# A fused attention and two-layer MoE kernel on one Trainium2 core: partial token sums kept as one running sum, a second double bank for scores, five buffers for float64 weights

## The chip, the core and the metric

The kernel runs on one core of one Trainium2 chip. TensorE (PE) multiplies, with a weight load (PEld) ahead of each matmul; VectorE (DVE), ScalarE (ACT) and GpSimd (POOL) do the elementwise work; SyncE (SP) issues every DMA of this kernel, one after the other in one queue. SBUF holds 128 partitions. PSUM has eight banks, into which PE writes; here a bank holds 512 float32 numbers in each partition. The metric is the device time of one execution in microseconds (us).

## The reference

Batch 4, 12 heads, 448 tokens, head size 64; the first expert layer is 768 x 2048, the second has 32 slots for 8 experts of 1024. All inputs are float32 but two: `w_in` and `w_out` carry a factor that numpy keeps in float64 and reach the kernel as 64-bit words.

```python
scores = scale * q @ k.T;  causal mask;  attn = softmax(scores);  x = attn @ v     # per head
x = concatenate the heads                                                         # [4*448, 768]
h = x @ w_in;  g = h * clip(h + 3, 0, 6) / 6;  y = g @ w_out                      # 768 -> 2048 -> 768
logits = y @ phi                                                                  # [1792, 32]
d = exp(logits - max over tokens) / (sum over tokens + 1e-9)
slot_input = d.T @ y                                                              # [32, 768]
slot_out[e] = maximum(slot_input[e] @ w1[e], 0) @ w2[e]                           # 8 experts, 4 slots each
c = softmax of logits over slots;  out = c @ slot_out                             # [1792, 768]
```

## The kernel before

**Stages.** Attention runs over 24 pairs of heads (6 for each batch). The first expert layer runs over 64 units, 16 feature tiles of 128 for each of the 4 batches: one unit is 18 matmuls (L734, both operands split into a high and a low part, three products of six row blocks), a ReLU on ACT (L739), a product on DVE (L741) and, for batches 1 to 3, a 32 x 32 block transpose (L745) into `gtok`, which holds a batch's `g`. `y` is never formed: `phi` is multiplied into `w_out` beforehand (`wp`), so four units at a time give logits (L767), and `d.T @ g` (`U`) is multiplied by `w_out` once, at the end.

**Float64 weights.** Each of 32 blocks of `w_out` and `w_in` is loaded as 64-bit words into one of three `raw` buffers, turned into float32 by ACT and three DVE operations (L627 to L639), and stored back to DRAM as float32 (`wo_d`, `wi_d`). Units of batches 1 to 3 load `wi_d`.

**Token sums.** For batch 0 `U` is a plain product (L939). For batches 1 and 2, 56 small matmuls of 512 columns (`ublocks`, L785) leave four partial sums in four PSUM banks, and four DVE operations add them to four partial sums in SBUF (`U4`, 128 x 2048), each scaled by `c1(SAL)`. After the last batch eight such DVE operations (L857) follow, and then, for eight pieces in turn, PE adds up and transposes the parts (L1045, L1049), DVE copies the piece to `wp` (L1054) and PE multiplies it by `w_out` (L1062).

**Second layer.** `w1` and `w2`, 64 loads of 768 KB, pass through buffers named `ring`. These are laid into SBUF as earlier stages leave it: `RINGS` says how many at each of eight points, in the order start, `cv_end` (conversions over), `a_end` (attention over), `b_end` (batch 2 over), `x_end` (last unit's weights read), `h_end` (last unit multiplied), `g_end` (users of the `g` buffers done), `m_end` (users of `gtok` done); five more come at `o_end`, when the product with `w_out` is done. A load that has no buffer holds up the SP queue behind it.

**Order.** The program has no fixed order: every step is put into a `Schedule` with engine, assumed cost, dependencies, buffers and a priority made from the table `TU`, and a list scheduler writes all instructions in the order it finds. It also writes throwaway matmuls (L390, `filler`) where it expects PE to be idle. PSUM: three `h` banks for units and logits, one double bank `ps` for scores (a pair needs it four times), one `o`, two `t` for transposes. Attention of batch 0 uses `t`; later pairs are transposed on DVE and by DMA (`xd`).

## Time and profile before

| | |
|---|---|
| runs | 656.09, 655.76, 654.37 us; median 655.76 |
| profiled execution | 655.37 us, of which the span is 653.5 |
| granted TensorE clock, mean | 0.958 |
| busy: PE, DVE, ACT, POOL | 594.8, 407.5, 250.4, 150.6 us |
| moved by DMA | 144.59 MB, mean 221 GB/s |

Busy times of engines overlap, so they don't add up to the span. Where an engine waits, the trace names the one that released it. PE busy also counts the throwaway matmuls. A granted clock of 1.00 is 2.4 GHz, 0.50 is 1.2 GHz.

### The profile page before, as it was taken

What the parts mean: (1) busy time and instruction counts of PE and PEld (TensorE: products, weight loads), DVE (VectorE), ACT (ScalarE), POOL (GpSimd) and SP (SyncE); (2) the same over time, 40 slices, a digit from 0 to 9 for tenths busy, and PEclk for the clock granted to TensorE, in tenths of its full rate; (3) what the DMA queues carried; (4) which work ended last, traced back from release to release, by engine and by line L of the source; (5) the groups of instructions that cost most, each with busy time, mean ns of one, the idle gap of its engine ahead of it and who ended that gap; (6) DMA issues with size and microseconds to landing.
All of it is one profiled execution on the core that took longest, in us unless ns stands there. A gap on an engine that the chain in (4) does not pass through costs nothing.

```text
span 653.5 us, 14639 instructions
## 1 busy us (share of the span) xinstructions
PE 594.8 (91%) x5816; PEld 446.1 (68%) x5816; DVE 407.5 (62%) x948; ACT 250.4 (38%) x420; POOL 150.6 (23%) x212
## 2 busy tenths in 40 slices
PE   7799899988988889999999999999999999998582
PEld 5688676766877678758878777888788654463021
DVE  6889888679886796787686867555655423010032
ACT  2466556445455554524344541433333201110032
POOL 1234446424462222323234322210000010000000
PEclk8899999899998999999999999999999999879877
DMA  7998878879879789872676543279833449999987
GB/s 205 314 294 254 217 213 207 189 168 241 171 199 252 171 194 249 219 168 76 121 164 125 135 91 79 73 206 402 314 97 97 174 175 416 415 414 414 393 291 252
DMA packets 196244, 144.59 MB, mean 221 GB/s; under 512 B 154704, under 2 KB 174672, under 8 KB 196176
## 3 DMA queue, kind: packets, MB, share of 16 engines
q1 hardware_dynamic: 196176, 143.66, 74.5%
q8 instruction: 46, 0.75, 0.5%
q14 instruction: 22, 0.18, 0.1%
HBM read 121.41 MB, written 22.22 MB: 220 GB/s over the span
## 4 chain that ended last, share of the span: by engine, by line
PE 45%; DMA 12%; DVE 10%; SPq 2%; ACT 2%; issue 2%; DVEq 0%; ACTq 0%
PE ph L734 25%; DMA ring<-in_moe_w_dram 8%; DMA raw<-in_moe_w_in_dram 3%; DVE ps L491 3%; PE ps L526 2%; SPq L406 2%; PE t L1124 2%; PE o L564 2%; PE pl L767 1%; PE t L785 1%; PE ps L1109 1%; PE pl L734 1%; PE ph L1109 1%; PE ps L476 1%; PE o L1062 1%
## 5 line engine op out<-in xcount | busy, mean ns | idle before, releaser
L734 PE MATMUL ph<-xp,wpl 128*128 128x448 f32 x1098 | 238.3, 372 | 2.4 <-DVE wpl L723 2.3
L734 PEld LDWEIGHTS ph<-xp,wpl 128*128 128x128 f32 x1098 | 204.0, 189 | 32.7 <-issue 8.7
L739 ACT ACTIVATE r<-ph,three 128x448 f32<-128x448 f32 x61 | 38.6, 632 | 124.0 <-PE ph L734 119.3
L549 POOL TENSOR_SCALAR_AFFINE_SELECT s<-s 128x256 f32<-128x256 f32 x96 | 49.6, 540 | 145.4 <-ACT s L541 140.1
L741 DVE SCALAR_TENSOR_TENSOR g<-r,ph 128x448 f32<-128x448 f32 x61 | 37.5, 614 | 55.4 <-ACT r L739 52.4
L491 DVE CUSTOM_DVE_ANT_0 ps<-ps,maskw 128x448 f32<-128x448 f32 (+3 forms) x144 | 61.7, 428 | 15.1 <-PE ps L476 10.5
L725 POOL TENSOR_TENSOR wpl<-cx,wpl 128x768 fp32r<-128x768 f32 x26 | 49.8, 1916 | 80.7 <-ACT wpl L720 74.8
L720 ACT ACTIVATE wpl<-cx 128x768 fp32r<-128x768 f32 x64 | 53.6, 838 | 29.6 <-PE ph L734 16.0
L526 PE MATMUL ps<-qp,kp 64*64 64x64 f32 (+3 forms) x576 | 58.2, 309 | 6.7 <-DVE mc L491 2.7
L541 ACT ACTIVATE s<-ps 128x896 f32<-128x896 f32 (+2 forms) x72 | 50.0, 731 | 28.6 <-PE ps L531 25.8
L526 PEld LDWEIGHTS ps<-qp,kp 64*128 64x128 f32 (+1 forms) x576 | 42.4, 177 | 22.5 <-ACT s L541 5.1
L564 PE MATMUL o<-vr,s 128*64 128x65 f32 (+1 forms) x1536 | 53.6, 224 | 0.0
L564 PEld LDWEIGHTS o<-vr,s 128*64 128x64 f32 (+1 forms) x1536 | 48.6, 137 | 5.0 <-issue 2.9
L627 ACT ACTIVATE ca<-raw 128x768 f32<-128x768 f32 x32 | 29.4, 919 | 46.8 <-DMA raw<-in_moe_w_in_dram 26.3
L723 DVE TENSOR_TENSOR wpl<-cx,wpl 128x768 fp32r<-128x768 f32 x38 | 35.8, 943 | 3.9 <-ACT wpl L720 3.6
L476 PE MATMUL ps<-kp,qp 64*128 64x448 f32 (+1 forms) x192 | 27.3, 342 | 11.5 <-DVE mc L495 4.0
L745 DVE STREAM_TRANSPOSE gtok<-g 128x448 f32<-128x448 f32 x48 | 29.7, 632 | 4.0 <-PE ps L785 3.1
L636 DVE SCALAR_TENSOR_TENSOR cw<-ca,cw 128x768 uint32<-128x768 uint32 x32 | 30.7, 958 | 2.2 <-ACT ca L627 0.7
L476 PEld LDWEIGHTS ps<-kp,qp 64*128 64x128 f32 x192 | 14.4, 173 | 23.9 <-issue 10.1
L630 DVE TENSOR_SCALAR cw<-raw 128x768 uint32<-128x768 uint32 x30 | 18.7, 622 | 19.0 <-DMA raw<-in_moe_w_in_dram 11.1
L531 PE MATMUL ps<-dg,oner 64*128 64x448 f32 (+1 forms) x192 | 28.4, 295 | 0.0
L1215 PE MATMUL o<-ring,wos 128*32 128x384 f32 x108 | 21.3, 627 | 5.7 <-DMA ring<-in_moe_w_dram 5.7
(236 smaller groups left out, 802.0 us busy)
## 6 DMA issues: line engine op xcount, KB each, us to landing
ring<-in_moe_w_dram SPq DMA_DIRECT2D x54, 768.0 KB, 14.6
cx<-wi_d SPq DMA_DIRECT2D x48, 384.0 KB, 3.5
...
wos<-in_moe_w_dram SPq DMA_DIRECT2D x10, 768.0 KB, 15.1
...
```

The source lines that it names most:

```text
L476: nc.tensor.matmul(ps.t[:n, h, c:c + w], pl["q"].t[r, 0, q0:q0 + n], pl["k"].t[r, 0, 0:w], start=(t == part[0][0]), stop=adds, skip_group_ ...
L491: nc.vector.tensor_tensor_reduce(out=x, in0=x, in1=maskw[:n, 320 - q0:320 + n] if t else maskw[:n, 320:320 + n], scale=-1.0, scalar=3.0e38 ...
L526: nc.tensor.matmul(ps.t[:kn, h, col:col + n], pl["k"].t[r, x, q0:q0 + kn], pl["q"].t[r, y, q0:S], start=(c == 0 and col == 0), stop=False, ...
L541: nc.scalar.activation(out=o, in_=x, func=ACTF.Exp, scale=SCALE)
L549: nc.gpsimd.affine_select(out=x, in_=x, pattern=[[0, 2], [1, kn]], compare_op=ALU.is_ge, fill=0.0, base=0, channel_multiplier=-1)
L564: nc.tensor.matmul(o.t[64 * h:64 * h + 64, VD * j:VD * j + VD], s.t[:kn, h, c:c + 64], vr.t[:kn, h, t, :], start=(t == 0), stop=(t == ts[- ...
L720: e = sc.add("ACT", 0.84, lambda w=w, cx=cx: nc.scalar.activation(out=w.t[:, 0], in_=cx.t, func=ACTF.Copy), [cr], [cx, w], ps_)
L723: ("DVE", 1.0, lambda w=w, cx=cx: nc.vector.tensor_sub(w.t[:, 1], cx.t, w.t[:, 0].bitcast(F32))),
L725: ("POOL", 2.0, lambda w=w, cx=cx: nc.gpsimd.tensor_sub(w.t[:, 1], cx.t, w.t[:, 0].bitcast(F32))),
L734: nc.tensor.matmul(h.t[:, :S], w.t[:, a, kk, :], x.t[:, c, kk, :], start=(n == 0), stop=(n == len(seq) - 1))
L739: rr = sc.add("ACT", 0.63, lambda h=h, r=r: nc.scalar.activation(out=r.t, in_=h.t[:, :S], func=ACTF.Relu, bias=three), [hh], [h, r], pr - ...
L741: gg = sc.add("DVE", 0.62, lambda h=h, r=r, g=g: nc.vector.scalar_tensor_tensor(out=g.t, in0=r.t, scalar=6.0, in1=h.t[:, :S], op0=ALU.min, ...
```

## The change

Three edits to the computation. (1) For batches 1 to 3 the four partial sums are copied to SBUF by ACT or DVE (into a part of `gtok` whose use is over), added up by four PE matmuls of `sel4`, and one DVE operation scales and adds the result into one running sum `U` (`collect`); `U4` is gone. For the last batch this is done in two halves of 256 columns; each half is then transposed on DVE straight into `wp`, and the product with `w_out` follows. Batch 0's `U` is brought into the same layout by four more PE transposes and three DVE operations. (2) The two `t` banks become one double tile `pt`; once all users of `t` are done it joins the pool `ps` as a second double bank. The logits are transposed to `ltok` by eight DVE transposes for a batch instead of PE transposes, for batches 1 to 3; the ReLU is written into `g`, so the pool `r` is gone. (3) `raw` has five buffers. `g_end` now waits for users of `g`, `zT` and `ls`. The scheduler is told the kind of each PE step (the whole array, `full`, or tiles of it), prefers a step of the kind last run (`KEEP`) and counts a turn between kinds (`TURN`); costs of loads and steps and most of `TU` have other values.

```diff
-TU = {'PO': [-130.96, -7.26, -2.82, -5.86], 'TO': [11.72, -10.42, 32.02, 147.16], 'PB': 0.63, 'AB': -1.38, 'TB': 194.0, 'DUTY': 0.6, 'RINGS': [1, 4, 2, 3, 1, 6, 2, 3], 'LOOK': 0.49, 'FILL': 0.96, 'RAW': 3, 'CA': 1, 'CW': 1, 'S': 2, 'PAIR': 12.99, 'UNIT': 4.99, 'WP0': 35.23, 'WPS': 7.75, 'T0': 216.97, 'L0': -2.47, 'L1': -0.16, 'GP': 201.12, 'TP': 4.91, 'ZP': 38.03, 'UP': 36.81, 'P0': 14.01, 'NQ': 2, 'WAIT': 0.09, 'AHEAD': 2.19, 'LAT': 0.23, 'CX': 2, 'G': 5, 'R': 1, 'VR': 2, 'XT': 2, 'Q': 1, 'AS': 1.42, 'A1': -27.02, 'A2': 6.86, 'A3': 17.6, 'A4': -15.86, 'A5': 3.85, 'A6': 27.35, 'A7': 16.05, 'DG': 2, 'DV': 6, 'TT': 2, 'LO': 1.77, 'DA': 6, 'DX': 6}
+TU = {'KEEP': 2.63, 'PO': [-133.04, -17.63, -10.01, -36.65], 'TO': [8.22, 2.26, 22.67, 165.17], 'PB': 0.68, 'AB': -0.37, 'TB': 219.67, 'DUTY': 0.6, 'RINGS': [0, 6, 2, 4, 1, 5, 2, 3], 'LOOK': 0.65, 'FILL': 0.96, 'RAW': 5, 'CA': 1, 'CW': 1, 'S': 2, 'PAIR': 12.84, 'UNIT': 4.71, 'WP0': 32.06, 'WPS': 6.3, 'T0': 212.76, 'L0': -15.91, 'L1': -14.62, 'GP': 199.53, 'TP': 0.97, 'ZP': 85.68, 'UP': 95.27, 'P0': 15.86, 'NQ': 2, 'WAIT': 0.09, 'AHEAD': 3.2, 'LAT': 0.23, 'CX': 2, 'G': 5, 'R': 1, 'VR': 2, 'XT': 2, 'Q': 1, 'AS': 1.42, 'A1': -10.9, 'A2': 7.25, 'A3': 45.16, 'A4': -24.35, 'A5': -8.06, 'A6': 29.73, 'A7': 16.15, 'DG': 2, 'DV': 6, 'TT': 2, 'LO': -17.05, 'DA': 6, 'DX': 6}
...
-                x = min((x for x in c if x[0] <= t0 + self.WAIT), key=lambda x: (x[1].prio, x[1].n))
+                x = min((x for x in c if x[0] <= t0 + self.WAIT), key=lambda x: (
+                    x[1].prio + (self.KEEP if x[2][1] == "PE" and x[1].full != self.full else 0.0), x[1].n))
...
-                cost = self.array(t, cost, s.weight)
+                cost = self.array(t, cost + (self.TURN if s.full != self.full else 0.0), s.weight)
+                self.full = s.full
...
-        many(mog, TU["R"], "r", [P, S])
...
-        ptt = many(pst, 2, "t", [P, 512])
+        ptt = pst.tile([P, 2, 512], F32, name="pt")
+        sc.pool("t", [ptt[:, 0], ptt[:, 1]])
...
-                h, r, g, x = sc.buf("h"), sc.buf("r"), sc.buf("g"), xb[b]
+                h, g, x = sc.buf("h"), sc.buf("g"), xb[b]
...
+                hh.full = True
+                rr = sc.add("ACT", 0.63, lambda h=h, g=g: nc.scalar.activation(
+                    out=g.t, in_=h.t[:, :S], func=ACTF.Relu, bias=three), [hh], [h, g], pr - TU["GP"])
+                gg = sc.add("DVE", 0.62, lambda h=h, g=g: nc.vector.scalar_tensor_tensor(
+                    out=g.t, in0=g.t, scalar=6.0, in1=h.t[:, :S], op0=ALU.min, op1=ALU.mult), [rr], [h, g], pr - TU["GP"])
...
-            def ublocks(banks, zT):
+            def ublocks(banks, zT, f0=0, nf=KF):
...
-                            banks[i][o:o + 32, :], zT.t[r, 32 * j:32 * j + 32], ug[r, :, 32 * j:32 * j + 32],
+                            banks[i][o:o + 32, :32 * nf], zT.t[r, 32 * j:32 * j + 32],
+                            ug[r, f0:f0 + nf, 32 * j:32 * j + 32],
...
+            def collect(banks, bufs, um, up, c0, n, deps, pr, v0=0):
+                part = gflat[:, c0:c0 + 4 * n].rearrange("p (i x) -> p i x", i=4)
+                ev = []
+                for i in range(4):
+                    ev.append(sc.any([
+                        ("ACT", 0.16 + n * 0.84e-3, lambda i=i: nc.scalar.activation(
+                            out=part[:, i], in_=banks()[i][:, :n], func=ACTF.Copy)),
+                        ("DVE", 0.1 + n * 1.04e-3, lambda i=i: nc.vector.tensor_copy(part[:, i], banks()[i][:, :n])),
+                    ], [um], bufs, pr))
+
+                def total():
+                    for i in range(4):
+                        nc.tensor.matmul(
+                            up()[32 * i:32 * i + 32, :n], sel4[:, 0, :], part[:, i],
+                            start=True, stop=True, tile_position=(0, 32 * i))
+
+                m = sc.add("PE", 0.2 + n * 1.7e-3, total, ev, bufs, pr)
+                return sc.add("DVE", 0.1 + n * 1.04e-3, lambda: nc.vector.scalar_tensor_tensor(
+                    out=U[:, v0:v0 + n], in0=U[:, v0:v0 + n], scalar=c1(SAL), in1=up()[:, :n],
+                    op0=ALU.mult, op1=ALU.add), [m] + deps, bufs, pr), ev
...
-                zT, idS = sc.buf("zT"), sc.buf("g")
...
-                ub, u2 = [sc.buf("t") for _ in range(2)], sc.buf("ps", False)
-                banks = lambda: [ub[0].t, ub[1].t, u2.t[:, 0], u2.t[:, 1]]
-                um = sc.add("PE", 3.7, lambda: ublocks(banks(), zT), [zd] + lasts, [gtb, zT, u2] + ub, T1)
+                ldone = logits_out(lr, [la], T1 + 2)
+                ua, ub = [sc.buf("ps") for _ in range(2)], [sc.buf("h") for _ in range(3)] + [sc.buf("o")]
                 u_part = []
-                for hf in range(2):
-                    cs = slice(8 * hf, 8 * hf + 8)
-
-                    def uadd(cs=cs):
-                        for i in range(4):
-                            nc.vector.scalar_tensor_tensor(
-                                out=U4[:, cs, i], in0=U4[:, cs, i], scalar=c1(SAL), in1=blk(banks()[i])[:, cs],
-                                op0=ALU.mult, op1=ALU.add)
-
-                    u_part.append(sc.add("DVE", 1.4, uadd, [um, sal, s0, prev_u], ub + [u2], T1 + hf))
+                for hf, bufs in enumerate((ua, ub)):
+                    def banks(hf=hf):
+                        return [u.t for u in ub] if hf else [u.t[:, x] for u in ua for x in range(2)]
+
+                    um = sc.add("PE", 2.2, lambda hf=hf, banks=banks: ublocks(banks(), zT, 8 * hf, 8),
+                                [zd] + lasts, [gtb, zT] + bufs, T1 + 3 * hf)
+                    u, ev = collect(banks, [gtb] + bufs, um, lambda banks=banks: banks()[0], hf * DFF * 7 // 4, 256,
+                                    [sal, prev_u], T1 + 3 * hf + 1, 256 * hf)
+                    u_part.append(sc.add("DVE", 0.38, lambda hf=hf: nc.vector.transpose(
+                        wp[:, 8 * hf:8 * hf + 8, :].rearrange("p f s -> p (f s)"), U[:, 256 * hf:256 * hf + 256]),
+                        [u], [], T1 + 3 * hf + 1))
+                    if not hf:
+                        si, si_free = ua[1], ev
...
+                ub = [sc.buf("ps") for _ in range(2)]
+                banks = lambda ub=ub: [u.t[:, x] for u in ub for x in range(2)]
+                bufs = [gtb] + ub
+                a = sc.add("PE", 4.3, lambda banks=banks, zT=zT: ublocks(banks(), zT), [zd] + lasts,
+                           [zT] + bufs, T0 + UNIT * KF - TU["UP"])
+                prev_u, _ = collect(banks, bufs, a, lambda ub=ub: ub[0].t[:, 0], 0, 512, [prev_stat, prev_u], pr)
...
+        def t_end():
+            sc.free["t"].clear()
+            sc.grant("ps", ptt)
+
+        sc.add("SP", 0.0, t_end, sc.users("t"), [], 0)
...
-        ge = sc.add("SP", 0.0, g_end, [he] + sc.users("g", "r", "ls"), [], 0)
+        ge = sc.add("SP", 0.0, g_end, [he] + sc.users("g", "zT", "ls"), [], 0)
...
-        si = sc.buf("o")
         smm = None
-        for hf in range(2):
-            for c in range(4):
-                up = sc.buf("h")
-                j0 = 2 * hf
-
-                def utr(up=up, c=c, j0=j0):
-                    nc.tensor.matmul(
-                        up.t[:, :64], U[:, c * P:(c + 1) * P], idS.t[:, 32 * j0:32 * j0 + 64],
-                        start=True, stop=False, skip_group_check=True)
-                    for j in range(2):
+        for m in range(KF // 2):
+            def simm(m=m):
+                for d in range(2):
+                    for r in range(2):
+                        g = d * 2 + r
                         nc.tensor.matmul(
-                            up.t[:, 32 * j:32 * j + 32], U4[:, 4 * (j0 + j) + c].rearrange("p i x -> p (i x)"),
-                            sel4[:, 0, :], start=False, stop=(j == 1), skip_group_check=True)
-
-                a = sc.add("PE", 0.4, utr, [u_part[hf]], [up, idS], T1 + 4 * hf + c)
-                a = sc.add("DVE", 0.16, lambda up=up, c=c, j0=j0: nc.vector.tensor_copy(
-                    uT[:, c, j0:j0 + 2], up.t[:, :64].rearrange("p (j s) -> p j s", s=NS)), [a], [up], T1 + 4 * hf + c)
-
-                def simm(c=c, hf=hf):
-                    f0 = c + 8 * hf
-                    for d in range(2):
-                        for r in range(2):
-                            g = d * 2 + r
-                            nc.tensor.matmul(
-                                si.t[32 * g:32 * g + 32, :384], uT[:, c, f0 // 4 + r, :],
-                                held["wo"][:, f0 + 4 * r, d * 384:(d + 1) * 384],
-                                start=(c == 0 and hf == 0), stop=(c == 3 and hf == 1), tile_position=(0, 32 * g),
-                            )
-
-                smm = sc.add("PE", 0.73, simm, [a] + wol + ([smm] if smm else []), [si], T1 + 4 * hf + c)
+                            si.t[32 * g:32 * g + 32, 0, :384], wp[:, 2 * m + r, :],
+                            held["wo"][:, 2 * m + r, d * 384:(d + 1) * 384],
+                            start=(m == 0), stop=(m == KF // 2 - 1), tile_position=(0, 32 * g),
+                        )
+
+            smm = sc.add("PE", 0.73, simm, [u_part[m // 4]] + (si_free if not m else [smm]) + wol, [si], T1 + 4 + m)
```

**PE, after the last unit.** L1045 and L1049 add up a piece, L1062 multiplies by `w_out`; `wos` holds `w_out`. Before:

```order
L1045 MATMUL ph0_252<-g4_196,U_81 128x64
L1049 MATMUL ph0_252<-sel4_74,U4_82 128x32 x2
L1062 MATMUL o0_256<-wos_5107,wp_79 32x384 x4
L1045 MATMUL ph1_253<-g4_196,U_81 128x64
L1049 MATMUL ph1_253<-sel4_74,U4_82 128x32 x2
L1062 MATMUL o0_256<-wos_5107,wp_79 32x384 x4
```

Now, with L788 the last small matmuls of the second half and L806 the adding up of the first and of the second half:

```order
L788 MATMUL pl_250<-gtok_186,zT0_193 32x256
L788 MATMUL o0_252<-gtok_186,zT0_193 32x256
L806 MATMUL ps0_251<-gtok_186,sel4_74 32x256 x4
L806 MATMUL ph1_249<-gtok_186,sel4_74 32x256 x4
L1059 MATMUL pt_253<-wos_4874,wp_79 32x384 x32
```

Pieces are no longer added up in turn between products; both halves of the small matmuls, 224 in place of 112 passes, stand ahead of all 32 products.

**SP, the last loads of 64-bit words.** `wi_d` is a store of a converted block, `xd` and `xt` the transposes of attention by DMA. Before:

```order
L406 DMA xd12_163<-xt0_240 64x7x64 x2
L406 DMA wi_d11_186<-cx1_205 128x768
L406 DMA raw0_245<-in_moe_w_in_dram 128x6x256
L406 DMA xt0_240<-xd12_163 32x14x32 x4
L406 DMA wi_d12_187<-cx0_204 128x768
L406 DMA raw1_246<-in_moe_w_in_dram 128x6x256
```

Now:

```order
L410 DMA xd10_156<-xt0_234 64x7x64 x2
L410 DMA wi_d11_181<-cx1_199 128x768
L410 DMA raw0_239<-in_moe_w_in_dram 128x6x256
L410 DMA wi_d12_182<-cx0_198 128x768
L410 DMA xt0_234<-xd10_156 32x14x32 x4
L410 DMA raw1_240<-in_moe_w_in_dram 128x6x256
```

The last load stands behind the store of pair 11 (xd10) instead of pair 13 (xd12); it still stands right behind the store of block 12.

**PE, late pairs of attention.** L564 (now L569) is a pair's product with `v`, L476 and L526 (now L481, L531) its scores, L734 a unit. Before, from pair 22 on:

```order
L564 MATMUL o0_256<-vr1_225,s1_233 64x65 x32
L476 MATMUL ps0_255<-kp1_231,qp1_229 128x448 x2
L476 MATMUL ps0_255<-kp1_231,qp1_229 64x64 x2
L734 MATMUL ph1_253<-xp0_200,wpl1_203 128x448 x18
L526 MATMUL ps0_255<-qp0_228,kp0_230 128x448 x6
L531 MATMUL ps0_255<-dg0_238,oner_210 128x448 x2
L526 MATMUL ps0_255<-qp0_228,kp0_230 64x64 x6
L531 MATMUL ps0_255<-dg0_238,oner_210 64x64 x2
L734 MATMUL ph0_252<-xp0_200,wpl0_202 128x448 x18
```

Now, pairs 22 and 23:

```order
L569 MATMUL o0_252<-vr1_219,s1_227 64x65 x32
L481 MATMUL ps0_251<-kp0_224,qp0_222 128x448 x2
L481 MATMUL ps0_251<-kp0_224,qp0_222 64x64 x2
L481 MATMUL pt_253<-kp0_224,qp0_222 128x192 x2
L481 MATMUL pt_253<-kp0_224,qp0_222 128x320 x2
L829 MATMUL ph0_248<-ls0_192,sel4_74 128x448
L569 MATMUL o0_252<-vr0_218,s0_226 64x65 x32
L739 MATMUL pl_250<-xp0_194,wpl1_197 128x448 x18
```

Scores use both double banks, and no unit stands between the products of pairs 22 and 23, where three stood before.

## Rows read from the trace of the kernel before

**Rows 1.** The page, part 1: busy us, share of span, instructions.

```profile
span 653.5 us, 14639 instructions
PE 594.8 (91%) x5816; PEld 446.1 (68%) x5816; DVE 407.5 (62%) x948; ACT 250.4 (38%) x420; POOL 150.6 (23%) x212
```

**Rows 2.** Windows: length, busy us of each engine, clock, DMA share, GB/s.

```profile
0.00:113.00 113.00, 100.97 (x1465) 80.37 (x1465) 93.15 (x192) 60.23 (x98) 43.54 (x86) 0.94 0.84 244
113.00:243.00 130.00, 115.63 (x1128) 94.54 (x1127) 104.98 (x243) 66.11 (x114) 47.97 (x56) 0.97 0.84 196
243.00:425.00 182.00, 178.92 (x1731) 144.66 (x1730) 131.07 (x345) 73.87 (x122) 55.43 (x69) 1.00 0.58 138
425.00:516.00 91.00, 91.00 (x549) 75.56 (x548) 49.28 (x77) 30.25 (x46) 1.86 (x1) 1.00 0.61 209
...
516.00:539.50 23.50, 21.88 (x267) 12.15 (x265) 8.62 (x28) 2.26 (x6) 1.80 (x1) 1.00 0.59 217
539.50:625.00 85.50, 71.89 (x616) 32.57 (x616) 10.93 (x47) 8.41 (x17) 0.00 (x0) 0.86 1.02 409
625.00:653.50 28.50, 14.49 (x68) 6.24 (x68) 9.48 (x18) 9.25 (x20) 0.00 (x0) 0.80 0.79 256
```

**Rows 3.** Timeline of SP: start, us of issuing, what is issued.

```profile
516.15 0.33 SPq L406 DMA_DIRECT2D ring<-in_moe_w_dram  x1
516.53 2.66 SPq L406 DMA_DIRECT2D ring<-in_moe_w_dram  x5
...
536.96 2.40 SPq L406 DMA_DIRECT2D ring<-in_moe_w_dram  x5
538.91 0.44 SPq L406 DMA_DIRECT2D ring<-in_moe_w_dram  x1
...
631.75 12.72 SPq L406 DMA_DIRECT2D out_dram<-ring  x8
```

**Rows 4.** Waits of SP, 500 to 545 us: in total, times, longest.

```profile
SPq L406 <- PE pl L1045: 15.1, 1, 15.1
```

**Rows 5.** Windows after the last unit, columns as in Rows 2.

```profile
527.00:529.00 2.00, 1.88 (x16) 1.74 (x16) 2.00 (x7) 0.00 (x0) 0.00 (x0) 1.00 1.02 421
529.00:531.00 2.00, 2.00 (x19) 1.30 (x18) 0.54 (x4) 0.00 (x0) 0.00 (x0) 1.00 0.12 46
...
535.00:537.00 2.00, 2.00 (x19) 1.33 (x19) 0.23 (x1) 0.00 (x0) 0.31 (x1) 1.00 0.00 0
```

**Rows 6.** The chain that ended last: start, us, what.

```profile
241.22 3.90 PE ph L734 x18
...
512.27 3.85 PE ph L734 x18
516.12 0.75 PE t L809 x2
...
521.51 0.62 PE t L785 x2
...
525.84 1.65 DVE U L857 x4
...
537.35 2.14 PE o L1062 x24
```

**Rows 7.** Groups by line: busy us, mean ns, idle before and its releasers.

```profile
L390 PE MATMUL ph<-ident 128*32 128x128 f32 x124 | 20.1, 296 | 0.0
...
L741 DVE SCALAR_TENSOR_TENSOR g<-r,ph 128x448 f32<-128x448 f32 x61 | 37.5, 614 | 55.4 <-ACT r L739 52.4 <-PE pl L767 3.0
...
L745 DVE STREAM_TRANSPOSE gtok<-g 128x448 f32<-128x448 f32 x48 | 29.7, 632 | 4.0 <-PE ps L785 3.1
...
L723 DVE TENSOR_TENSOR wpl<-cx,wpl 128x768 fp32r<-128x768 f32 x38 | 35.8, 943 | 3.9 <-ACT wpl L720 3.6
```

**Rows 8.** Waits, 113 to 243 us: columns as in Rows 4.

```profile
DVE cw L630 <- DMA raw<-in_moe_w_in_dram: 10.6, 4, 3.9
```

More of the change, by code (lines that the diff above doesn't have):

```diff
@@ L28, in __init__ @@
         self.weight = 1.0
+        self.full = False
         self.next = []
@@ L50 @@
     ISSUE = 0.65
+    TURN, KEEP = 0.157, TU["KEEP"]
     TICK, ENTRY = 10.24 / 3, 3072 / 2400
@@ L58, in __init__ @@
         self.fill = None
+        self.full = False
         self.cols = {}
@@ L451, in attention @@
                     a = sc.add("PE", 0.5, tr, [l], [tp, buf, dst], p0)
+                    a.full = True
                 a.weight = 0.3
@@ L1010, in q_open @@
                 sc.grant("q", t)
+            for x in range(2):
+                sc.grant("t", ptt[:, x])
             sc.grant("acc0", pto[0])
```

106 lines of the change are left out of this document (40 added, 66 removed).

## The prediction, made before the changed kernel was run

> **What bounds the kernel now.** I read the page first, then the span in stages, then the waits and the chain at the stage borders. PE is busy for 91% of the span [rows 1], but the stages differ [rows 2]. Until 243 us (unit 16 has been multiplied shortly after) nothing is full: PE 100.97 of 113 and 115.63 of 130 us, throwaway matmuls among it, DVE 93.15 and 104.98, DMA 0.84. From 243 to 516 us PE is full: 178.92 of 182 and 91.00 of 91. From 539.5 to 625 us DMA is: 1.02 of it at 409 GB/s. The last 28.5 us are products and stores of the output. So the time is three terms: when the last unit ends (512.27 + 3.85 = 516.12, [rows 6]), how long the remaining `ring` loads take from there, and the output.
>
> **The stream of weights after the last unit.** SP issues six loads at 516.15 to 516.53 (h_end) and then none until 536.96 [rows 3]: it waits 15.1 us for PE L1045 [rows 4]. In the code that is g_end: its buffer held the scaled identity that L1045 reads, and L1045 stands in turn with the products L1062, the last of which ends at 537.35 + 2.14 [rows 6]. DMA runs out of work meanwhile: 421 GB/s at 527 to 529 us, 46 at 529 to 531, 0 at 535 to 537 [rows 5]. After 536.96 it is full to the end. So whatever moves the start of that stream moves the end as much.
>
> The change lets g_end wait for the small matmuls of the second half instead (last user of zT), m_end for the collecting, and only o_end for the products. When are they? The small matmuls began 521.51 - 516.12 = 5.4 us after the last unit and took until 525.84, 4.3 us [rows 6]. They have the same columns in two halves, so 4.3 if columns set the time; with twice the passes at the old price for each, 8.6. I take 5, since 112 passes in 4.3 us are 39 ns each, and 512 columns alone would be 213 ns at 2.4 GHz: tiles overlap, and columns and issuing both have a share. The ACT copy of logits in front of the maximum goes (a row of half a us at most); I leave it in the range. So g_end comes 5.4 + 5 = 10.4 us after the last unit (9.7 to 14.0). The five loads of h_end take 5 x 1.92 = 9.6 us (786432 bytes at 409 GB/s, [rows 2]). DMA then waits 0.5 us (0 to 4). The two loads of g_end give 3.8 us; copying four half banks, adding up and scaling are some 2 us (a 256-column DVE operation is 1.65/4 = 0.41 us, [rows 6]), so m_end is in time. The three of m_end give 5.8 more, to 10.9 + 3.8 + 5.8 = 20.5 us. Thirty-two products take 8 x 0.71 = 5.7 us (three pieces of four in 2.14, [rows 6]), so o_end comes at 10.4 + 2 + 5.7 = 18.1, before DMA runs dry. In bad cases (14.0 + 2 + 6.3 = 22.3 against 14.0 + 9.6 = 23.6) also.
>
> `RINGS` gives 1+4+2+3+1 = 11 loads ahead of the last unit's end before, 0+6+2+4+1 = 13 now. So 51 loads remain at that point instead of 53. Before, at 536.96, 20.84 us after the last unit, 64 - 17 = 47 remained. Now 51 remain at 0.3 us with a pause of 0.5. The stream ends earlier, counted from the last unit, by 20.84 - 0.3 - 0.5 - 4 x 1.92 = **12.4 us** (8.9 to 12.9). PE is no obstacle: it waits for DMA in that stage (71.89 of 85.5 us busy, at a clock of 0.86, [rows 2]), and the experts' products start where o_end did, 2 to 5 us earlier. The loads' own order and the output's are unchanged.
>
> The Trainium skill speaks against this at two places. "TensorE: Matmul & The Clock Gate" (Wait — 56ns, not 53.3ns?) says that starts are never closer than about 25 ns however few columns; 224 passes would then be an estimated 5.6 us, so the pause 1.1 and this term 11.8. No row has the half width; the 39 ns for 512 columns allow it. "DMA: Bandwidth & Descriptors" (Specifications) gives a core about 358 GB/s from HBM; a load would take an estimated 2.2 us and the term 11.3. The row of 409 GB/s disagrees, and I go by the row.
>
> **The time until the last unit.** The order now has 44 throwaway matmuls ahead of the last unit instead of 82 (two passes each; 124 passes in 20.1 us, [rows 7], so 38 fewer are 76 x 0.16 = 12 us of PE). They stand where the scheduler expected idleness, so this is no gain by itself, but it shows that the new order expects less of it, above all after the first unit. The turns between whole-array and tiled steps ahead of the last unit are 151 instead of 159, worth under 2 us. Added on PE: collecting for batches 1 and 2 and the four transposes for batch 0; gone: transposes of logits. Both are about 2 us; I count nothing for them and one us to either side.
>
> What moves is the mix. Before, 15 pairs were finished ahead of unit 16, now 12, and the last load of 64-bit words stands two pairs earlier in SP's queue. So two to three pairs, I take 2.3, leave the stage in which PE isn't full and go into the one where it is. A pair costs PE, in the full stage: 178.92 us less 26 units at (91.00 - 4.3)/22 = 3.94 and 10 for sums is 66 us for 8.5 pairs, 7.8 at most, and 6.5 if turns belong to units. It costs DVE there 131.07 - 26 x (0.61 + 0.63 + 0.943 x 38/64) = 84 us less 5 for sums, over 8.5: 9.3 us [rows 2, 7]. In the early stage DVE is busy 81%, so a pair takes up to 9.3/0.81 = 11.5 us there, and no less than 6.5. I take 10.5: 2.3 x (10.5 - 6.5) = 9 us won (0 to 11).
>
> Some is given back. By the 20th pair both orders stand at unit 29. Then four pairs come with 6 units in place of 13: on DVE 4 x 9.3 + 6 x 1.8 = 48 us, on PE 4 x 6.5 + 6 x 3.94 = 50. Six diagonals moved from DVE to POOL and the second double bank loosen this; but where DVE and PE want the same time, each waits for the other at times. I count 4 us lost there (0 at best, 9 if that stretch runs at DVE's 81%: 48/0.81 = 59).
>
> The five `raw` buffers I count as nothing. DVE waited 10.6 us for such loads from 113 to 243 us [rows 8], but in the new order the last loads still stand right behind the store of the block three earlier, and SP waits there for that conversion whatever the number of buffers. If the wait went, up to 10.6 us could.
>
> So the last unit ends 9 - 4 = **5 us** earlier (22 earlier, with raw waits gone too, to 9 later).
>
> **The sum.** 655.37 us of the profiled execution (653.5 of it the span) - 12.4 - 5 = 638.0; it lies 0.4 below the median shown, so 638.4.
>
> **Rivals.**
> A. Only the tail moves: pairs cost as much in the early stage as later, or the late pairs give back what was won. For it: DMA has the same 0.84 in both early stages [rows 2], and loads, not PE, may set them. Against it: DVE and PE are both off full there. 655.8 - 12.4 = 643.4.
> B. The early stage loses most of its idleness. PE was idle 12.0 + 14.4 us in it beside the throwaway matmuls [rows 2]. With earlier units to fill these gaps and raw waits gone, 20 us from the last unit: 655.8 - 12.4 - 20 = 623. Against it: single-banked scores remain until `t` is free, near pair 14.
> C. Slower: late attention becomes DVE's. If the six pairs from the 18th on ran at the first stage's pace of 113/7.5 = 15 us each instead of 182/8.5 = 21 less 3 units, 9, the last unit would end 6 x 6 = 36 us later, less the 9 won, and the tail gives 12.4: 671. It decides from 21 us of lost time on; below that the kernel is no slower. For it: the 48 against 50 us above. Against it: DVE had 51 us to spare in that stage [rows 2], and the stage of 91 us behind it has more.
> D. The tail doesn't move: m_end or o_end comes so late that DMA pauses again, say 8 us. Then 4.4 of the term is left: 655.8 - 4.4 - 5 = 646. Nothing in the rows speaks for such a late o_end but the pieces' old order.
>
> **How the numbers follow.** Forecast 0.52 (630 to 644), A 0.17, B 0.16, C 0.07, D 0.08. Predicted 638.4. The range takes in A and D and the near half of B: 625 to 650. What this kernel's measurement can tell from no change is 0.3%, 2 us. Faster by more: 0.92 (all but C and bad ends of D); within: 0.03; slower: 0.05.
>
> **What would show it.** In the profile after: SP's wait for PE after the last unit under 5 us, and DMA above 400 GB/s from the end of the last unit through the products with `w_out` but for a pause under 4 us; the first store of output some 17 us earlier than 631.75 [rows 3], with the same 22 us from there to the end. The last unit should end near 511, unit 16 near 221 instead of 241.22 + 3.90 = 245 [rows 6] with DVE over 80% until then, and PE idle for a few us between pairs 20 and 24. It is wrong in the tail if DMA pauses near the products, wrong in the early stage if unit 16 ends where it did, and wrong in the late pairs if PE idles there for over 10 us.

## The result, and the profile after

The changed kernel took 638.96 us (median of four runs, 633.69 to 640.88) beside 655.92 for the kernel before (654.37 to 659.50): a ratio of 0.9721, 95% interval 0.9651 to 0.9792. Predicted were 638.4, and 625 to 650. The total is right; its two terms are not. The tail gave 8.4 us instead of 12.4, the time until the last unit 6.5 in the profiled execution (640.88 us, span 639.2) instead of 5, and more in most others; that the sum came out within a us is luck.

The page after, part 1 (answers to [rows 1]):

```profile
PE 579.5 (91%) x5824; PEld 436.2 (68%) x5824; DVE 399.8 (63%) x909; ACT 254.1 (40%) x429; POOL 160.8 (25%) x242
```

Shares are as before; less work, not more overlap, is what the page shows: PE is busy 15.3 us less, of which 10.6 are throwaway matmuls (below). Where, the milestones tell. Units and pairs were counted by the ends of their matmuls in the traces. Eight profiles have the changed kernel's order on every engine but SP until batch 2 is over, so their spread is what one execution differs from another by.

| end of | before, two profiles | changed, profile | eight profiles of its order |
|---|---|---|---|
| unit 1 | 117.1, 119.4 | 106.5 | 105.4 to 110.7 |
| unit 16 | 252.9, 254.5 | 224.7 | 221.1 to 226.6 |
| pair 20 (29 units done, in both) | 342.2, 343.3 | 334.5 | 326.2 to 335.6 |
| unit 48 (24 pairs done, in both) | 446.2, 447.6 | 434.6 | 426.3 to 435.7 |
| last unit | 516.1, 517.5 | 509.6 | 499.1 to 509.6 (seven) |
| first store, after the last unit | 115.6 | 107.3 | |

The prediction set unit 16 at 245 in the kernel before; that was unit 15, and unit 16 ended at 252.9. Windows of before, then of after, cut at these milestones (columns as in Rows 2):

```profile
0.00:342.20 342.20, 313.84 (x3524) 252.47 (x3524) 273.66 (x645) 168.47 (x280) 121.48 (x175) 0.97 0.80 204
342.20:446.20 104.00, 102.89 (x901) 85.45 (x902) 66.40 (x151) 39.17 (x62) 27.30 (x37) 1.00 0.51 132
446.20:516.10 69.90, 69.90 (x443) 57.30 (x443) 38.42 (x61) 22.82 (x35) 0.00 (x0) 1.00 0.55 194
```

```profile
0.00:334.50 334.50, 307.14 (x3486) 248.82 (x3486) 265.25 (x612) 171.71 (x286) 140.14 (x212) 0.95 0.81 210
334.50:434.60 100.10, 100.10 (x873) 82.82 (x874) 69.46 (x153) 38.53 (x61) 15.24 (x27) 1.00 0.67 189
434.60:509.60 75.00, 72.71 (x448) 57.17 (x447) 37.43 (x60) 23.16 (x36) 3.66 (x2) 0.98 0.38 127
```

The first stage is 7.7 us shorter at the same PE share, the second 3.9 with PE full, the third 5.1 longer: PE waits 2.3 us there for `zT` of batch 2. Pair 20 is not quite the same point in both: the changed kernel has run one pair's scores more by then (L526 and L531 before, L531 and L536 now). From there to unit 48, before and then after:

```profile
L526 PE MATMUL ps<-qp,kp 64*128 64x448 f32 (+3 forms) x96 | 9.4, 302 | 0.8 <-DVE mc L491 0.7
```

```profile
L531 PE MATMUL ps<-qp,kp 64*128 64x448 f32 (+1 forms) x36 | 3.6, 302 | 0.0
L531 PE MATMUL pt<-qp,kp 64*128 64x320 f32 (+1 forms) x36 | 3.4, 298 | 0.0
```

That is 96 passes in 9.4 us before and 72 in 7.0 now, and of the other line 32 in 4.6 and 24 in 3.5. So up to 3.5 of the 3.9 us were won ahead of pair 20. The throwaway matmuls of the first stage, before and after:

```profile
L390 PE MATMUL ph<-ident 128*32 128x128 f32 x124 | 20.1, 296 | 0.0
L390 PE MATMUL pl<-ident 128*32 128x128 f32 x24 | 3.9, 278 | 0.0
```

```profile
L393 PE MATMUL ph<-ident 128*32 128x128 f32 x62 | 11.4, 326 | 0.0
L393 PE MATMUL pl<-ident 128*32 128x128 f32 x12 | 2.0, 279 | 0.0
```

Of 24.0 us 13.4 are left, while PE's idle time, 342.2 - 313.84 = 28.4 us, is now 27.4. So idleness and filling together fell by some 12 us, while more scores were run; DVE gave 8.4 us of work up, and POOL took 18.7.

The tail. Timeline of SP (answers to [rows 3]), and what SP and PE waited for (to [rows 4]):

```profile
509.66 2.55 SPq L410 DMA_DIRECT2D ring<-in_moe_w_dram  x5
523.48 2.94 SPq L410 DMA_DIRECT2D ring<-in_moe_w_dram  x5
...
616.91 13.14 SPq L410 DMA_DIRECT2D out_dram<-ring  x8
```

```profile
SPq L410 <- PE o L788: 7.8, 1, 7.8
...
PE pl L788 <- issue: 2.5, 1, 2.5
PE ps L788 <- DVE zT L858: 2.3, 1, 2.3
```

The second group of loads comes 13.8 us after the last unit, not 10.4. The chain shows why (answers to [rows 6]):

```profile
505.72 3.91 PE ph L739 x18
509.63 0.75 PE pl L829 x2
...
513.80 0.30 DVE ltok L820
...
514.19 0.73 ACT ls L850 x2
514.95 0.66 DVE zT L858
...
520.36 2.46 issue
...
525.14 4.77 PE pt L1059 x56
```

The transposes of logits now stand ahead of the exponential, so the small matmuls start 6.0 us after the last unit; 220 of 224 are done 4.7 us later, and then PE stands 2.46 us on "issue": it waits for nothing that the profile shows. A window of L788 alone (length, busy us of PE and PEld, clock, DMA share, GB/s), and what DMA did then (answers to [rows 5]):

```profile
515.65:520.36 4.71, 4.71 (x220) 3.58 (x220) 1.00 1.01 421
```

```profile
519.00:521.00 2.00, 1.36 (x69) 0.80 (x48) 0.45 (x2) 0.45 (x2) 0.00 (x0) 1.00 0.93 380
521.00:523.00 2.00, 0.18 (x2) 0.14 (x4) 0.00 (x0) 0.00 (x0) 0.00 (x0) 1.00 0.04 9
523.00:525.00 2.00, 1.82 (x20) 0.64 (x16) 1.27 (x3) 0.66 (x2) 0.00 (x0) 1.00 0.49 52
525.00:527.00 2.00, 1.86 (x24) 0.81 (x28) 0.90 (x3) 0.00 (x0) 0.28 (x1) 1.00 0.78 310
```

Some 3.5 us are lost, where 0.5 was forecast, and the pause of before (529 to 537 us in [rows 5]) is gone otherwise.

### The profile page after: what moved, and what is told of

It reads as the page before. It is cut to its first block, busy times and chain, and to the rows that moved or that the text cites. A ratio compares the mean times of both kernels' runs of the same rounds, so it can differ in the third digit from the quotient of the medians.

```text
span 639.2 us, 14659 instructions
## 1 busy us (share of the span) xinstructions
PE 579.5 (91%) x5824; PEld 436.2 (68%) x5824; DVE 399.8 (63%) x909; ACT 254.1 (40%) x429; POOL 160.8 (25%) x242
## 4 chain that ended last, share of the span: by engine, by line
PE 45%; DMA 14%; DVE 3%; SPq 2%; issue 1%; ACT 1%; POOL 1%; DVEq 0%; ACTq 0%
PE ph L739 19%; DMA ring<-in_moe_w_dram 9%; PE pl L739 8%; PE o L569 4%; DMA wos<-in_moe_w_dram 2%; SPq L410 2%; PE ps L531 2%; DMA cx<-wi_d 1%; PE ps L788 1%; PE pt L531 1%; DMA xt<-xd 1%; PE ph L773 1%; PE pt L938 1%; PE ps L481 1%; PE pt L1059 1%
## 5 line engine op out<-in xcount | busy, mean ns | idle before, releaser
L739 PE MATMUL ph<-xp,wpl 128*128 128x448 f32 x846 | 183.8, 371 | 1.5 <-POOL wpl L730 1.5
L739 PEld LDWEIGHTS ph<-xp,wpl 128*128 128x128 f32 x846 | 156.2, 188 | 26.9 <-ACT g L745 5.9
L745 ACT ACTIVATE g<-ph,three 128x448 f32<-128x448 f32 x47 | 29.7, 633 | 101.2 <-PE ph L739 101.2
L739 PE MATMUL pl<-xp,wpl 128*128 128x448 f32 x306 | 66.7, 371 | 0.0
L739 PEld LDWEIGHTS pl<-xp,wpl 128*128 128x128 f32 x306 | 56.7, 188 | 7.1 <-issue 1.8
L747 DVE SCALAR_TENSOR_TENSOR g<-g,ph 128x448 f32<-128x448 f32 x47 | 28.9, 616 | 51.7 <-ACT g L745 51.6
L569 PE MATMUL o<-vr,s 128*64 128x65 f32 (+1 forms) x1536 | 55.3, 228 | 0.0
L569 PEld LDWEIGHTS o<-vr,s 128*64 128x64 f32 (+1 forms) x1536 | 50.2, 141 | 5.8 <-issue 3.2
L531 PE MATMUL ps<-qp,kp 64*128 64x448 f32 (+2 forms) x468 | 47.2, 309 | 4.0 <-DVE rc L581 2.3
L496 DVE CUSTOM_DVE_ANT_0 ps<-ps,maskw 128x448 f32<-128x448 f32 (+3 forms) x108 | 46.2, 428 | 7.2 <-PE ps L481 2.3
L531 PEld LDWEIGHTS ps<-qp,kp 64*128 64x128 f32 (+1 forms) x468 | 34.4, 175 | 16.1 <-issue 5.7
L481 PE MATMUL ps<-kp,qp 64*128 64x448 f32 (+3 forms) x156 | 23.5, 356 | 12.5 <-DVE mc L496 5.4
L481 PEld LDWEIGHTS ps<-kp,qp 64*128 64x128 f32 (+1 forms) x156 | 12.2, 180 | 20.7 <-issue 7.8
L635 DVE TENSOR_SCALAR cw<-raw 128x768 uint32<-128x768 uint32 x26 | 18.7, 720 | 7.9 <-DMA raw<-in_moe_w_in_dram 7.0
```

What stands on the lines that cost most here:

```text
L481: nc.tensor.matmul(ps.t[:n, h, c:c + w], pl["q"].t[r, 0, q0:q0 + n], pl["k"].t[r, 0, 0:w], start=(t == part[0][0]), stop=adds, skip_group_ ...
L496: nc.vector.tensor_tensor_reduce(out=x, in0=x, in1=maskw[:n, 320 - q0:320 + n] if t else maskw[:n, 320:320 + n], scale=-1.0, scalar=3.0e38 ...
L531: nc.tensor.matmul(ps.t[:kn, h, col:col + n], pl["k"].t[r, x, q0:q0 + kn], pl["q"].t[r, y, q0:S], start=(c == 0 and col == 0), stop=False, ...
L569: nc.tensor.matmul(o.t[64 * h:64 * h + 64, VD * j:VD * j + VD], s.t[:kn, h, c:c + 64], vr.t[:kn, h, t, :], start=(t == 0), stop=(t == ts[- ...
L739: nc.tensor.matmul(h.t[:, :S], w.t[:, a, kk, :], x.t[:, c, kk, :], start=(n == 0), stop=(n == len(seq) - 1))
```

## Experiments

**1. The early release alone, in the kernel before.**

```diff
-                zT, idS = sc.buf("zT"), sc.buf("g")
+                zT = sc.buf("zT")
-                s0 = sc.add("DVE", 0.2, lambda: nc.vector.tensor_scalar_mul(idS.t[:, 0:P], ident, c1(SAL0)), [s0], [idS], T1 + 1)
+                s0 = sc.add("DVE", 0.62, lambda: nc.vector.tensor_scalar_mul(U, U, c1(SAL0)), [s0, prev_u], [], T1 + 1)
...
-                        up.t[:, :64], U[:, c * P:(c + 1) * P], idS.t[:, 32 * j0:32 * j0 + 64],
+                        up.t[:, :64], U[:, c * P:(c + 1) * P], ident[:, 32 * j0:32 * j0 + 64],
...
-        ge = sc.add("SP", 0.0, g_end, [he] + sc.users("g", "r", "ls"), [], 0)
+        ge = sc.add("SP", 0.0, g_end, [he] + sc.users("g", "r", "ls", "zT"), [], 0)
```

> The kernel before with one edit after its last unit: U is scaled in place (one DVE operation of 512 columns) instead of a scaled identity in a g buffer, so g_end waits for the small matmuls (end 525.84 in the trace of before) and no longer for the products. Up to the last unit the order is the same. Theory, the stream of ring loads sets the end: six loads last until 529, five more (g_end, m_end) until 538.8, o_end still near 539.5, so 42 loads remain at 539.5 where 47 remained at 536.96: 5 x 1.92 - 2.5 = 7.1 us sooner, 648.7. Rival, a gap of PE under full DMA as in the kernel after (2.5 us) also comes here and delays o_end: 4.6 us, 651. Rival, the release is not what sets the end: 655.8.

646.90 us, ratio 0.9871 (0.9802 to 0.9940). SP issues five loads 9.8 us after the last unit, and DMA has no pause (SP's timeline; its wait; two of six windows, of which none falls under 402 GB/s):

```profile
527.30 2.24 SPq L406 DMA_DIRECT2D ring<-in_moe_w_dram  x5
...
624.52 12.97 SPq L406 DMA_DIRECT2D out_dram<-ring  x8
```

```profile
SPq L406 <- PE ps L785: 4.4, 1, 4.4
```

```profile
529.00:531.00 2.00, 2.00 (x20) 1.94 (x24) 1.77 (x7) 0.00 (x0) 0.00 (x0) 1.00 1.05 418
...
537.00:539.00 2.00, 2.00 (x20) 1.11 (x23) 0.45 (x2) 0.00 (x0) 0.00 (x0) 1.00 1.04 421
```

First store 107.0 us after the last unit: 8.6 of 115.6 us won by one wait less, as much as the change wins in its tail. (The changed kernel has two loads fewer left after the last unit as well, some 3.8 us, but frees the next buffers 4.0 us later than this one.) No "issue" wait came with these 112 passes. The mechanism is shown.

**2. The release held back in the changed kernel.** The edit is `[he, smm]` in place of `[he]` in `ge`.

> The changed kernel with g_end (and so m_end) waiting for the products with w_out too, as the kernel before did; the order up to the last unit is the same. Theory, the early release is what the tail gained from: DMA, which runs dry near 521.2, stands until the products end at 530.3 instead of 524.7, so about 6 us slower than the changed kernel, 645 (the pause in the trace 9 to 10 us instead of 3.5). Rival, the gain is all from the order ahead of the last unit: no change, 638.4.

638.41 us, ratio 0.9765 (0.9669 to 0.9861), so the total shows no difference. The first store came 109.9 us after the last unit, 2.6 later, not 6. The edit moved only the order in SP's queue. What a load waits for is the last use of its memory, and the memory of the first two was free after the small matmuls as before:

```profile
503.28 14.63 SPq L410 DMA_DIRECT2D ring<-in_moe_w_dram  x7
521.62 4.05 SPq L410 DMA_DIRECT2D wos<-in_moe_w_dram  x5
525.77 1.81 SPq L410 DMA_DIRECT2D ring<-in_moe_w_dram  x3
```

Seven loads came ahead of the products instead of ten. So this tells less than experiment 1; it fits it (three loads later, 2.6 us lost).

**3. The last batch in one piece.**

```diff
-                for hf, bufs in enumerate((ua, ub)):
...
-                    um = sc.add("PE", 2.2, lambda hf=hf, banks=banks: ublocks(banks(), zT, 8 * hf, 8),
-                                [zd] + lasts, [gtb, zT] + bufs, T1 + 3 * hf)
...
+                um = sc.add("PE", 3.7, lambda: ublocks(banks(), zT), [zd] + lasts, [gtb, zT] + ua, T1)
+                u, si_free = collect(banks, [gtb] + ua, um, lambda: ua[0].t[:, 0], 0, 512, [sal, prev_u], T1 + 1)
```

> The changed kernel with the last batch in one piece: 112 small matmuls of 512 columns in place of 224 of 256 after the last unit, then one collecting of 512 columns and two transposes. Theory, PE's gap of 2.5 us there comes from the number of instructions (448 used up in 4.7 us, PE waiting for its own program): with 224 no gap, small matmuls 4.3 us as in the kernel before, g_end at 10.4 us after the last unit instead of 13.85, no pause of DMA, 3.4 us sooner, 635. Rival, the gap belongs to the place or to the full DMA and not to the number: gap stays, g_end at 12.8, 1 us sooner, 637.5. Rival, the longer collecting makes o_end late (20 us and more after the last unit): no gain or slower, 638 to 641.

633.87 us, ratio 0.9627 (0.9534 to 0.9720); first store 104.9 us after the last unit. The wait on "issue" is gone, as the theory has it. The matmuls still took 5.9 us, not 4.3: after the wait for `zT` the granted clock was 0.50 for a while, and DMA still paused (226 and 129 GB/s from 516 to 520 us). So the first store is 2.4 us sooner, not 3.4; the rest of the 5 us between the two medians is not the tail's.

```profile
512.00:514.00 2.00, 2.00 (x60) 0.81 (x65) 0.57 (x3) 0.00 (x0) 0.00 (x0) 0.82 1.01 424
514.00:516.00 2.00, 2.00 (x58) 1.23 (x33) 0.00 (x0) 0.00 (x0) 0.00 (x0) 0.50 1.04 433
```

**4. DMA idle during the small matmuls.** Two tries. In the first, `RINGS` gave the five loads of h_end to g_end.

> The changed kernel with the five ring loads of h_end given at g_end, so that DMA has one load to do while the small matmuls run. If PE's gap of 2.5 us comes of the program's own blocks waiting behind 768 KB loads, it is gone: the small matmuls end 10.8 us after the last unit instead of 13.6, and the time is 5 x 1.92 - 3 = 6.6 us longer, 645. If the blocks come too slowly for 224 short passes whatever DMA does, the gap stays, the matmuls end at 13.6, and the time is 9.6 us longer, 648.

631.06 us in one run; but the loads still came at the end of the last unit, since their memory is what h_end frees. It says nothing on the question and is a repeat of the changed kernel (last unit at 499.1, first store 107.7 later, 1.4 us of "issue"). In the second, that memory stays unused:

```diff
-            rings(RINGS[5])
+            take("pad", [P, 5 * RING])
```

> The changed kernel with five ring buffers fewer: their memory stays unused from h_end on, so that DMA has one load to do after the last unit and is idle while the 224 small matmuls run. If PE's gap of 2.5 us there comes of blocks of its program waiting behind 768 KB loads, it is gone: the small matmuls end 10.8 us after the last unit instead of 13.8. If the blocks come too slowly for 448 short instructions whatever DMA does, the gap stays and they end at 13.8. The time is longer by some 5 x 1.92 = 10 us less the 3 in the first case.

645.87 us in one run, first store 115.1 us after the last unit. No wait on "issue" is left with the same 224 passes. The packet of PE's program (q8 is a queue of instructions; in the whole run it has 46 packets of 16 KB, one for some 253 of PE's 11,648 matmuls and weight loads) falls into these windows, in the changed kernel 10.4 to 11.9 us after the last unit, here 8.3 to 9.8, with next to nothing beside it:

```profile
q1 hardware_dynamic: 66, 0.31, 52.7%
q8 instruction: 1, 0.02, 4.1%
```

```profile
q8 instruction: 1, 0.02, 4.5%
```

The passes ended 12.4 us after the last unit, though, not 10.8, at a granted clock of 0.50 for a while:

```profile
514.80:516.80 2.00, 2.00 (x71) 1.82 (x61) 0.10 (x1) 0.00 (x0) 0.00 (x0) 0.50 0.03 8
```

The start of this packet in the other traces tells more. In the four profiles that share the changed kernel's order here (it and experiments 2, 7 and the first of 4) it lies 10.7 to 11.2 us after the last unit, when 184 to 220 of the passes have run; with DMA idle it lies at 8.5, after 106. And in all seven profiles with the gap PE goes on 2.3 to 2.6 us after the packet's start, though it had stood 1.4 to 3.0. So PE stood for a block of its program, and that block came later beside full DMA. The same 2.4 us after 8.5 are 10.9, an estimate from these numbers, and 220 passes at a granted clock of 1.00 are done at 10.7: idle DMA alone would have left little of the gap. That rests on one profile.

**5. The second double bank only after attention.** The edit is `sc.users("t") + att_all` in `t_end`'s step.

> The changed kernel with the tile pt given to the pool of scores only when attention is over, so that scores have one double bank throughout, as before; the order is the same until pt would have joined (pair 15 or so). From the end of pair 20 to the end of unit 48 the kernel before took 104.0 and the changed one 100.1 us. Theory, the second bank is what made the late pairs cheaper: the last unit ends 4 us or more later (508 instead of 504, the mean of four profiles of the order of the changed kernel), PE idle several us between pairs 15 and 24, time 643. Rival, the late pairs are cheaper because there is less work for PE (turns, transposes of logits): 638, as the changed kernel.

677.72 us (671.48 to 683.21), ratio 1.0266 (1.0171 to 1.0362): over 30 us more than the changed kernel in every run, far beyond what the theory had. A window over the last pairs, in the execution of 683.21 us:

```profile
340.00:430.00 90.00, 79.42 (x1006) 64.32 (x1006) 54.16 (x157) 26.83 (x44) 19.08 (x40) 1.00 0.51 103
```

PE is idle 10.6 us there. But the edit does two things: batch 1's sums need both double banks too, so they waited for the end of attention (they start at 422.1 us, in the changed kernel at 377.4), and the units of batch 2 came late (unit 32 ended at 334.7, unit 36 at 397.2, unit 40 at 443.2). The order depends on that bank; its worth for scores alone isn't separated. Nor is much of the 3.9 us between 104.0 and 100.1 left for it to explain, as the passes of scores above show.

**6. Undoing parts that the order depends on.** The table of before in the new code (`TU` as before, KEEP 0); three `raw` buffers (`'RAW': 3`); no preference for a kind (`TURN, KEEP = 0.0, 0.0`).

> The code of the changed kernel with the table of the kernel before (three raw buffers, RINGS and all priorities of before, KEEP 0): seven pairs stand ahead of the first unit and 15 ahead of unit 16, as before. Theory, the part ahead of pair 20 was won by the order of the table, the rest by the code: unit 16 ends near 252 as before (224 in the changed kernel), the last unit near 512, first store 107 to 108 us after it, time 655.8 - 8.4 - 4 = 643. Rival, the code (second bank, five raw buffers apart) wins it all: 638. Rival, the code's gain depends on the table altogether (its sums and banks come at wrong times): 647 and more, last unit at 516.

> The changed kernel with three raw buffers instead of five, everything else of table and code as changed (the scheduler then finds another order: 13 pairs ahead of unit 16 instead of 12). Theory of the prediction, the number of raw buffers is worth nothing by itself: unit 16 ends some 9 us later for the one pair more, the rest evens out, 638 to 642. Rival, the earlier loads are what lets the units start sooner: unit 16 ends near 245, the last unit 6 us or more later, 645 and more.

> The changed kernel with the preference for a step of the kind last run and the cost of a turn set to nothing (KEEP and TURN 0), the table else the same; 85 throwaway matmuls instead of 44 ahead of the last unit, and 13 pairs ahead of unit 16 instead of 12. Theory, the preference itself is worth what turns cost, under 2 us, but this table was made with it, so the order gets worse: 645, last unit near 511. Rival, it makes no difference: 638. Rival, the turns cost much more than thought: 650 and more.

655.14 us, 0.9959 (0.9917 to 1.0000); 654.68, 0.9959 (0.9924 to 0.9995); 648.97, 0.9884 (0.9815 to 0.9953). The last unit ends at 521.7, 522.1 and 517.8, unit 16 at 251.7, 238.0 and 248.6. In each the scheduler finds another order, and each loses all that was won ahead of the last unit, whichever was undone (the first two end the last unit 4 to 6 us later than the kernel before); the tail stays (first store 108.0, 108.7 and 109.4 us after it). With three buffers the conversions did not wait longer for loads (18.4 us of ACT and DVE together from 100 to 345 us, 23.2 in the changed kernel); PE waited longer for DVE's maxima in that stretch. The two lines, three buffers and then five:

```profile
PE ps L481 <- DVE mc L496: 15.3, 6, 4.3
```

```profile
PE ps L481 <- DVE mc L496: 5.4, 2, 3.9
```

So the gain of that part belongs to the one order that was made for all numbers together. The table of the changed kernel in the code of before wasn't tried.

**7. The wait ahead of batch 2's sums.** First the four loads of b_end behind these sums (`[ae, h_last[B - 2], sums]` in `be`).

> The changed kernel with the four ring loads of b_end standing behind the sums of batch 2 in SP's queue (three of them stood ahead of a load of cx, which then took 8.89 us instead of some 3.4); PE, DVE and ACT keep their order until the last unit. Theory, that cx load made ACT and with it zT late, so that PE stood 2.3 us ahead of the sums of batch 2 and then ran at a lower clock: from the end of unit 48 to the end of the last unit 70 us (69.9 in the kernel before) instead of 73.4 (72.6 to 75.0 in four profiles), 3.4 us sooner, 635. Rival, zT is late for another reason (the order on DVE and ACT): 73 us again, 638.

636.93 us, 0.9665 (0.9592 to 0.9739), and 73.1 us from unit 48 to the last: the rival holds. The load of `cx` was sooner, and so was POOL's subtraction behind it, which now ran beside DVE's maximum (POOL; DVE):

```profile
443.14 1.84 POOL L730 TENSOR_TENSOR wpl<-cx,wpl 128x768 fp32r<-128x768 f32 x1 [55.74 <-ACT wpl L725]
```

```profile
443.55 1.45 DVE L881 TENSOR_TENSOR st<-st 128x1 f32<-128x1 f32 x1
...
445.11 1.21 DVE L820 STREAM_TRANSPOSE ltok<-ph 32x128 f32<-32x128 f32 x4
```

A DVE operation on one column took 1.45 us, to the end of POOL's; then the transposes hold the exponential up by 1.2. One delay took another's place: PE still waits 1.9 us for `zT`, 2.3 in the changed kernel.

**8. The best of these together.** One piece, the loads behind the sums, and the last batch's transposes behind `zT` (`[zd]` for `[la]` in `logits_out`); then those of batches 1 and 2 too.

> The changed kernel with three edits: the last batch in one piece of 112 small matmuls (first store 104.93 us after the last unit in its run, against 107.28), the transposes of its logits behind the one of zT (1.2 us sooner for the small matmuls), and the four ring loads of b_end behind the sums of batch 2. Theory, the three add up: 2.35 + 0.5 to 1 + 3.4 = 6.5 us under the changed kernel, 632; first store 104 us after the last unit, TensorE's clock at 1.00 in the small matmuls since the wait ahead of them is shorter. Rival, DMA already has no pause with one piece, so the sooner zT gives nothing: 632.7. Rival, the loads moved behind the sums are missed by the experts: 634 to 636.

> The combined kernel (one width, loads behind sums) with one more edit: the four transposes of batch 2's logits stand behind the one of zT, not ahead of the exponential. Theory, they hold up the exponential by 1.2 us there as they did after the last unit, so PE waits 1.1 us less for zT ahead of the sums of batch 2; from the end of unit 48 to the end of the last unit 71 to 72 us instead of 73.1, time 631. If the shorter wait also spares the drop of the clock in the sums (0.69 there), 70 us and 629.5. Rival, zT is late by the DVE operation on the maximum alone (1.45 us beside a subtraction on POOL): 73 again, 632.5.

632.52 us, 0.9615 (0.9552 to 0.9677), and 630.33, 0.9610 (0.9569 to 0.9651). In the first the small matmuls start 4.9 us after the last unit, the wait for `zT` is 1.2 us, the clock stays at 1.00 and they take 4.3; DMA has no pause, and the first store comes 102.8 us after the last unit:

```profile
511.90:513.90 2.00, 1.97 (x66) 0.97 (x68) 1.74 (x8) 0.00 (x0) 0.00 (x0) 1.00 1.03 430
513.90:515.90 2.00, 2.00 (x63) 1.01 (x46) 0.00 (x0) 0.00 (x0) 0.00 (x0) 1.00 1.01 424
```

In the second, PE's wait ahead of batch 2's sums is gone, and unit 48 to the last takes 71.1 us. The scheduler also gave that subtraction to DVE, so the one-column operation took 0.16 us there; the two causes aren't told apart. Both are faster than the kernel before. Their medians lie below the changed kernel's 638.96, too; the interval of the first overlaps with its 0.9651 to 0.9792, that of the second just meets it.

## Why the prediction was right, and where it was not

*The tail, 12.4 forecast, 8.4 measured, outside its own 8.9 to 12.9.* The mechanism is shown by experiment 1. The step that failed is "I take 5" for the small matmuls, with the start at 5.4. They started at 6.0, because four transposes that I had not placed stand ahead of the exponential (experiment 8: 4.9 without them); 220 of 224 passes took 4.7 us, as forecast; then came 2.46 us of "issue" that no row of before shows. So g_end came at 13.8 instead of 10.4, near the late end of the given 9.7 to 14.0, and DMA paused 3.5 us instead of 0.5. With the measured 13.85 the prediction's own formula gives 20.84 - 13.85 + 1.92 = 8.9 us, the 1.92 for one load fewer that remains (46 for 47). It takes DMA as full from there on; it was 0.49 and 0.78 busy until 527 us, so 8.4 were left. The other steps held: the loads of `wos` at o_end were issued 18.4 us after the last unit (18.1), then the stream ran full, and the output took 22.3 us. Of the signs named, SP's wait is 7.8 us instead of under 5 and the first store 14.8 us sooner instead of 17, while the pause stays under 4.

On the two places in the Trainium skill: its page "TensorE: Matmul & The Clock Gate" (Wait — 56ns, not 53.3ns?) gives about 25 ns as the least time from start to start, by estimate 5.6 us or more for 224 passes. The row of 220 of them above is 4.71 us, 21 ns each, on tiles in turn; the trace disagrees. The about 358 GB/s for a core in the Trainium skill's "DMA: Bandwidth & Descriptors" (Specifications) are half of what a stack gives two cores, as the page derives them; this kernel runs on one core, and windows with DMA full have 402 to 433 GB/s. (The 11.3 us worked out from that price kept a pause of 0.5 us, for which loads of 2.2 us leave no room; without it the term is 11.7.)

*The last unit, 5 us earlier forecast, 6.5 in the profile, 6.5 to 17 over seven profiles, 10 in their median.* Three steps stand behind it. "2.3 x (10.5 - 6.5) = 9 us won" came out at 7.7 up to pair 20 (7 to 16 over the profiles), or up to 11 with the scores that the changed kernel had run ahead. Unit 16 ended at 224.7 us, 28 sooner, where 221 was named from a start that was unit 15's.

"I count 4 us lost" for the late pairs is the step that failed: nothing was lost there. The stretch is 3.9 us shorter (100.0 to 100.2 us in all eight profiles, for 104.0 and 104.3), most of it the one pair's scores that had been run before. What was mis-sized is the cost of a pair in the full stage, 6.5 us of PE and 9.3 of DVE. It was got by subtraction with 26 units and 8.5 pairs from 243 to 425 us. The trace of before has more work there: 509 of L734's matmuls are 28 units of 18, L564 is the products with `v` of ten pairs (64 passes each), L526 the scores of nine (24 each):

```profile
L734 PE MATMUL ph<-xp,wpl 128*128 128x448 f32 x491 | 107.2, 372 | 0.0
L564 PE MATMUL o<-vr,s 128*64 128x65 f32 (+1 forms) x640 | 22.3, 224 | 0.0
L526 PE MATMUL ps<-qp,kp 64*128 64x448 f32 (+3 forms) x216 | 21.2, 302 | 0.9 <-DVE mc L491 0.7
...
L734 PE MATMUL pl<-xp,wpl 128*128 128x448 f32 x18 | 3.9, 371 | 0.0
```

The same subtraction then gives (178.92 - 28 x 3.94 - 10)/9.5 = 6.2 us of PE where it had 7.8, and (131.07 - 28 x 1.8 - 5)/9.5 = 8.0 of DVE where it had 9.3. The window after, from pair 20 to pair 24:

```profile
334.50:377.50 43.00, 43.00 (x507) 36.48 (x516) 37.99 (x105) 19.52 (x33) 13.39 (x26) 1.00 0.70 135
```

It holds six units, four pairs' products and three pairs' scores. PE never waits (a few us of idleness were forecast), and the 48 us of DVE against 50 of PE of rival C were 38 against 43.

And "I count nothing" for the sums failed the other way: 2.6 to 5.1 us were lost behind unit 48. PE waits 1.3 to 2.3 us for `zT` of batch 2. The work grew by 1.2 us, of which the matmuls of collecting (L806) are 1.1: without the wait (the second kernel of experiment 8) the stretch takes 71.1 us for 69.9. And in the profiled execution alone the granted clock was 0.69 from 450 to 455 us, in the sums behind the wait. In the profiled execution the errors nearly cancel.

*`raw`, counted as nothing.* For the number of buffers that holds: from 100 to 345 us DVE and ACT waited 5.9 and 17.3 us for these loads with five, and 4.4 and 14.0 with three (experiment 6). But the kernel before waited 11.1 and 26.3, so a part of the wait went with the new order, which the prediction had not counted on. As an input to the scheduler five buffers were needed, like every other number of the table that was undone. That the order as a whole carries the gain was not among my steps; I had read two of its symptoms, fewer throwaway matmuls and fewer pairs ahead of unit 16.

*The rivals.* A, only the tail moves, is refuted by the milestones, C (its terms add up to 670, not 671) by the 43.00 us. B, more idleness lost, is half true: 12 us of idle and filled time went. D, a late m_end or o_end, did not come: o_end was at 18.4 us, and the pause of 3.5 us was g_end's. Which part of the table does it ahead of the last unit is open.
